# The routing of the second and third sequence begins one step later in the attention's list of steps

## The chip, the core and the metric

The kernel runs on one core of one Trainium2 chip. The metric is the device time of one execution in microseconds (us), the median of the runs. TensorE is called PE here, VectorE DVE, ScalarE ACT, GpSimd POOL and SyncE, whose queue issues most loads, SP.

## What is computed

Four sequences of 768 tokens with 8 heads of 64 go through windowed attention with four sink tokens. The result, 3072 rows of 512, goes through a mixture of 8 experts of which each token takes one, and then through one wide layer for all tokens. Cut to what matters:

```python
scores = scale * np.matmul(q, k.transpose(0, 1, 3, 2))
scores = np.where(is_sink | in_window, scores, -1000000000.0)
a = np.exp(scores - max); a = a / (sum + 1e-09)
x = np.matmul(a, v)                       # (4, 8, 768, 64) -> (3072, 512)

logits = x @ w_gate + modality_bias[modality_id]
e_idx = np.argmax(logits, axis=1)         # one of 8 experts for each token
out[mask] = gate_w[mask, None] * (np.maximum(x[mask] @ w1[e], 0.0) @ w2[e])

h = out @ w_in
out = (h * np.clip(h + 3.0, 0.0, 6.0) / 6.0) @ w_out
```

## The kernel before

**Stages.** The attention of 32 heads (4 sequences of 8) comes first and ends at about 225 us, the expert slots follow to about 590 us, and the wide layer fills the rest. All matmuls of the last two stages are TensorE's. The order on PE, DVE, ACT and POOL is the order in which the program writes the instructions; each engine works through its own list.

**A head.** `attend(n)` writes the steps of three heads at once: the scores of head n in three groups of two blocks (`scores_mm`, line 247), their maxima on DVE (`scores_max`, lines 261 to 272) and exponentials on ACT (`scores_exp`, lines 280 and 283); the transposes of head n-1's probabilities in two groups of three (`p_transpose`, line 318) with copies on ACT (`p_copy`, line 333) and masks on POOL; and the values of head n-2 (`values_mm`, lines 351 to 356). The normalisation of head n-3 (lines 361 to 373) stands inside the first maximum. Line 324 transposes a small block of sink values into the fourth quarter of the first group's buffer, and ACT copies that on line 328.

**Free slots.** Between the steps `attend` leaves six empty places (`None`). They are: ahead of the second scores, ahead of the first two values, ahead of the next two, ahead of the third scores, ahead of the last two values, and at the end of the head. At each of them one entry is taken from each of three lists: `side` (routing), `early` (start-up), `slow` (weights of the first expert and the first gather).

**Routing.** `route(b)` returns the routing of sequence b as a list of entries, each a list of small functions. `start(b)` puts that list into `side`, from the slot on that comes next; what is left of the former sequence's list is merged entry by entry. It is called ahead of heads 11, 19 and 27 for sequences 0, 1 and 2 and behind the loop for sequence 3. For each of the six blocks of 128 tokens the list has `txa` (four transposes of the attention's output `xb` on PE, line 393), one entry later `txb` (copy on ACT, line 398), one later `txc` (DVE subtracts the copy from the original, line 402); a block starts every three entries. `lga` are the gate's matmuls (line 410), `lgb` and `lgc` turn the result, `lgd` and `t1` to `t4` make the one-hot and gate value on DVE (lines 428 to 449, the one-hot on 443), `rk` counts ranks on PE (lines 456 and 459), `t5` and `t6` turn them into places (lines 464 to 470), `sx` and `keep` scale and store the rows (lines 476 to 483), `sc` scatters token numbers from POOL (line 494).

**The buffers.** `p_transpose`, `txa` and later the gathered rows' transposes (line 764) all write to tiles named `tp` of pool `pt`, which has two buffers in PSUM. A tile can be written when all readers of the one before in its buffer are done: ACT's copies of lines 333 and 328 for a `p_transpose`, ACT's copy of line 398 and DVE's subtraction of line 402 for a `txa`.

**Behind the loop.** What is left in `side` and `slow` becomes `rest`, of which six entries are taken at each step of the first expert slots. Line 701 is the second half of splitting a weight into a high and a low part (line 699 the first), on DVE or POOL; line 736 gathers token rows from POOL; lines 782 and 803 are the experts' matmuls.

Of the kernel before, what the change touches and what calls it, by code (L numbers as in the profile page):

```python
# [54 lines left out]
class Net:  # L55
# [321 lines left out]
    def route(self, b):  # L377
# [3 lines left out]
        q = []  # L381
# [118 lines left out]
        q = [[] for _ in range(ROUTED + late + 2 + 5 * (3, 2, 3, 1)[b])]  # L500
# [8 lines left out]
        for i in range(NB):  # L509
            q[33 + (1 if b == B - 1 else 2) * i].append(on(sx, i))  # L510
            q[(34 if b == B - 1 else 35) + (1 if b == B - 1 else 2) * i].append(on(keep, i))
            q[ROUTED + late + 1 + (3, 2, 3, 1)[b] * i].append(on(sc, i))
        return q

    def spread(self, places, n, most, move):

# [1147 lines left out]
```

## Time and profile before

| | us |
|---|---|
| median of 3 runs | 1120.08 |
| the runs | 1115.91 to 1120.35 |
| the profiled execution | 1115.64 |
| its span, first to last instruction | 1113.8 |
| PE busy | 1077.7 (97%) |
| DVE busy | 480.9 (43%) |
| ACT busy | 454.0 (41%) |
| POOL busy | 256.3 (23%) |

The span is cut into stretches to see where PE does not work. A row of the timeline is one instruction or several equal ones in a row, with the start, the duration and, in brackets, how long the engine was idle before it and what is thought to have ended that. PE's instructions overlap, so a group of them may end after the next has begun.

### The profile page before, as it was taken

The numbers are of one execution on the slowest core, as the hardware profiler recorded it, in microseconds if no ns is written. First come the engines' busy times: TensorE is split into PE (matmuls) and PEld (weight loads), VectorE is DVE, ScalarE is ACT, GpSimd is POOL, SyncE is SP. The second block draws the span as 40 slices with busy tenths as digits, with TensorE's granted clock in tenths as the row PEclk, the third lists the DMA queues.
The fourth block names the chain that finished last, engine by engine and source line by source line (L and its number), as shares of the span: only waits on it lengthen the run. The fifth ranks groups of instructions, "written<-read, shape, count | busy, mean of one in ns | idle before, by whom it ended". The sixth has DMA issues, their size and how long they took to land.

```text
span 1113.8 us, 18248 instructions
## 1 busy us (share of the span) xinstructions
PE 1077.7 (97%) x6805; PEld 988.8 (89%) x6805; DVE 480.9 (43%) x1271; ACT 454.0 (41%) x1111; POOL 256.3 (23%) x458
## 2 busy tenths in 40 slices
PE   8999999899999999999999999999999999999995
PEld 5998888798999987999988998989989989899894
DVE  5766869655544543742242422413314224133240
ACT  4555656544265645633252422413314224143140
POOL 3333536436142533442031000000000000000000
PEclk9999999999999999999999999999999999999998
DMA  6333778515786996772341010110101100100000
GB/s 189 107 111 90 161 152 165 106 57 106 152 241 187 268 278 218 174 193 87 64 124 38 21 38 10 30 38 8 31 10 30 38 11 29 33 7 20 10 11 22
DMA packets 59890, 102.07 MB, mean 92 GB/s; under 512 B 17552, under 2 KB 34576, under 8 KB 59792
## 3 DMA queue, kind: packets, MB, share of 16 engines
q1 hardware_dynamic: 39966, 74.16, 25.5%
q0 software_dynamic: 5840, 13.13, 4.8%
q10 hardware_dynamic: 13986, 13.53, 4.8%
q8 instruction: 55, 0.90, 0.4%
q14 instruction: 43, 0.35, 0.1%
HBM read 72.87 MB, written 27.92 MB: 90 GB/s over the span
## 4 chain that ended last, share of the span: by engine, by line
PE 56%; DVE 0%; DMA 0%; SPq 0%; issue 0%; POOL 0%; POOLq 0%; ACT 0%; DVEq 0%; ACTq 0%
PE mm L1084 24%; PE mm L1062 24%; PE mm L803 4%; PE mm L782 3%; DMA stg<-w_d 0%; PE tp L764 0%; DVE ga L1052 0%; SPq L1033 0%; DVE u L1067 0%; DVE ot L1090 0%; POOL out_dram L1098 0%; POOLq L1486 0%; DVE h L785 0%; ACT r L1065 0%; DVE cve L905 0%
## 5 line engine op out<-in xcount | busy, mean ns | idle before, releaser
L1062 PEld LDWEIGHTS mm<-yh,w 128*128 128x128 f32 x2304 | 274.6, 189 | 3.8 <-DVE u L1067 3.0
L1062 PE MATMUL mm<-yh,w 128*128 128x256 f32 x2304 | 275.0, 281 | 2.8 <-DVE u L1067 2.8
L1084 PE MATMUL mm<-w,ga 128*128 128x512 f32 x936 | 220.6, 394 | 0.1
L1084 PEld LDWEIGHTS mm<-w,ga 128*128 128x128 f32 x936 | 175.2, 188 | 39.9 <-DVE u L1067 0.3
L1065 ACT ACTIVATE r<-mm,b 128x256 f32<-128x256 f32 x192 | 91.2, 475 | 247.1 <-PE mm L1062 246.6
L803 PE MATMUL mm<-h,w 128*128 128x400 f32 x768 | 152.0, 351 | 2.4 <-POOL apart L493 2.2
L782 PE MATMUL mm<-xT,w 128*128 128x400 f32 x768 | 144.8, 347 | 2.0 <-ACT hT L842 1.6
L803 PEld LDWEIGHTS mm<-h,w 128*128 128x128 f32 x768 | 139.2, 190 | 4.1 <-POOL apart L493 2.6
L782 PEld LDWEIGHTS mm<-xT,w 128*128 128x128 f32 x768 | 139.7, 188 | 3.5 <-ACT hT L842 1.8
L1067 DVE SCALAR_TENSOR_TENSOR u<-r,mm 128x256 f32<-128x256 f32 x192 | 80.8, 421 | 140.0 <-ACT r L1065 139.6
L1098 POOL DMA_INDIRECT out_dram<-ot,idt x24 | 23.1, 962 | 491.4 <-ACT ot L1092 368.9
L1090 DVE COPY ot<-mm 128x512 f32<-128x512 f32 x12 | 8.3, 691 | 222.0 <-PE mm L1084 222.0
L247 PE MATMUL s<-kz,qq 128*128 128x260 f32 (+1 forms) x384 | 94.8, 369 | 4.6 <-ACT pr L283 2.6
L283 ACT ACTIVATE pr<-s,mn 128x132 f32<-128x132 f32 x160 | 52.3, 369 | 68.7 <-DVE mn L272 29.0
L701 POOL TENSOR_TENSOR w<-stg,w 128x512 fp32r<-128x512 f32 x35 | 47.1, 1350 | 131.3 <-ACT w L699 121.6
L247 PEld LDWEIGHTS s<-kz,qq 128*128 128x128 f32 x384 | 61.9, 191 | 10.2 <-ACT pr L283 3.3
L785 DVE SCALAR_TENSOR_TENSOR h<-mm,h 128x400 fp32r<-128x400 f32 x64 | 36.7, 573 | 74.1 <-ACT h L784 68.6
L1052 DVE SCALAR_TENSOR_TENSOR ga<-u,ga 128x256 fp32r<-128x256 f32 x156 | 67.2, 431 | 0.0
L1051 ACT ACTIVATE ga<-u 128x256 fp32r<-128x256 f32 x156 | 63.8, 409 | 1.1 <-DVE u L1067 1.1
L354 PE MATMUL o<-vt,pt5p 128*128 128x66 f32 x320 | 61.9, 275 | 0.0
L353 PE MATMUL o<-vt,pt5d 128*128 128x66 f32 x320 | 60.6, 271 | 0.0
L784 ACT ACTIVATE h<-mm 128x400 fp32r<-128x400 f32 x64 | 32.1, 502 | 69.7 <-PE mm L782 60.2
(228 smaller groups left out, 1236.9 us busy)
## 6 DMA issues: line engine op xcount, KB each, us to landing
stg<-w SPq DMA_DIRECT2D x16, 512.0 KB
cv<-w_in SPq DMA_DIRECT2D x16, 512.0 KB
w_d<-cva SPq DMA_DIRECT2D x32, 256.0 KB
cv<-w_out SPq DMA_DIRECT2D x16, 512.0 KB
stg<-w_d SPq DMA_DIRECT2D x16, 512.0 KB
yT_d<-y ACTq DMA_DIRECT2D x8, 800.0 KB
vt<-vv SPq DMA_DIRECT2D x16, 396.0 KB
kz<-kE SPq DMA_DIRECT2D x32, 197.0 KB
```

The source lines that it names most:

```text
L247: nc.tensor.matmul(s[:, a, :n], q[:, b], k[:, c:c + n], start=True, stop=True)
L283: self.nc.scalar.activation(pr[:, i], s[:, a, P:P + W], AF.Exp, bias=mn[:, i:i + 1], scale=-1.0)
L353: mm(o[:, j], d[:, j - 1], vt[:, j], start=False, stop=False)
L354: mm(o[:, j], p[:, j - 1], vt[:, j - 1], start=False, stop=False)
L782: nc.tensor.matmul(ph[:, :T1], w(k)[:, wi, c], xT[:, xi, k], start=(n == 0), stop=(n == 11))
L803: nc.tensor.matmul(py[:, :T1], wf[:, wi], h[:, hi, f], start=(n == 0), stop=(n == 23))
L1051: nc.scalar.mul(g(0, f), u, 1.0 / 6.0)
L1052: nc.vector.scalar_tensor_tensor(g(1, f), u, 1.0 / 6.0, g(0, f).bitcast(F32), ALU.mult, ALU.subtract)
L1062: nc.tensor.matmul(ph[:, :T2], w, yh[:, b, k], start=(n == 0), stop=(n == 11))
L1065: nc.scalar.activation(r, ph[:, :T2], AF.Relu, bias=self.b3)
L1067: nc.vector.scalar_tensor_tensor(u, r, 6.0, ph[:, :T2], ALU.min, ALU.mult)
L1084: nc.tensor.matmul(po, g(a, f)[:, t * P:(t + 1) * P], w[:, b], start=(n == 0), stop=(n == 47))
```

## The change

`route(b)` returns its list with one empty entry in front for sequences 1 and 2. The lists of sequences 0 and 3 are as they were.

```diff
-        return q
+        return [[]] * (b in (1, 2)) + q
```

All routing steps of the two sequences so move to the next free slot. The number of instructions of every engine is the same.

PE, head 20, the second head of sequence 1's routing (`kz_144` are its keys). Before:

```order
L247 MATMUL s<-kz_144,qq 128x128
L247 MATMUL s<-kz_144,qq 128x260
L318 MATMUL tp<-ident,pr 128x128 x3
L324 MATMUL tp<-ident,sk 128x128
L393 MATMUL tp<-ident,xb 128x128 x4
L247 MATMUL s<-kz_144,qq 128x260 x2
L318 MATMUL tp<-ident,pr 128x128 x3
```

After:

```order
L247 MATMUL s<-kz_144,qq 128x128
L247 MATMUL s<-kz_144,qq 128x260
L318 MATMUL tp<-ident,pr 128x128 x3
L324 MATMUL tp<-ident,sk 128x128
L247 MATMUL s<-kz_144,qq 128x260 x2
L318 MATMUL tp<-ident,pr 128x128 x3
L393 MATMUL tp<-ident,xb 128x128 x4
```

The four transposes of an even block have moved behind the second scores and the second group of probability transposes. Those of the odd block move in the same way from ahead of the third scores to behind them.

DVE, from head 19 into head 20 (`xt` is the routing's split copy, `mn` the maxima of the scores). Before:

```order
L402 TENSOR_TENSOR xt<-tp,xt 128x4x128
L361 TENSOR_SCALAR rc<-o 128x6
L261 ISA t_1930,mn<-s,m_165 128x128
L261 ISA mn 128x1
L366 RECIPROCAL rc<-rc 128x6
L373 TENSOR_TENSOR xb<-o,rc 128x6x64
L265 COPY_PREDICATED s<-up,s 128x128
L266 TENSOR_REDUCE mn<-s 128x1
```

After:

```order
L361 TENSOR_SCALAR rc<-o 128x6
L261 ISA t_1929,mn<-s,m_165 128x128
L261 ISA mn 128x1
L366 RECIPROCAL rc<-rc 128x6
L373 TENSOR_TENSOR xb<-o,rc 128x6x64
L265 COPY_PREDICATED s<-up,s 128x128
L266 TENSOR_REDUCE mn<-s 128x1
L402 TENSOR_TENSOR xt<-tp,xt 128x4x128
```

The subtraction for the odd block has moved behind the whole first maximum and normalisation of head 20.

ACT, from head 27 into head 28, with the split of an expert's weights (line 699). Before:

```order
L398 CAST xt<-tp 128x4x128
L283 ACTIVATE pr<-s,mn 128x132 x2
L398 CAST xt<-tp 128x4x128
L699 CAST w<-stg 128x512
L280 ACTIVATE pr<-t_2710,mn 128x128
```

After:

```order
L398 CAST xt<-tp 128x4x128
L283 ACTIVATE pr<-s,mn 128x132 x2
L699 CAST w<-stg 128x512
L398 CAST xt<-tp 128x4x128
L280 ACTIVATE pr<-t_2709,mn 128x128
```

The copy for the odd block has moved behind the weight cast that followed it.

## Rows read from the trace of the kernel before

**Rows 1.** Page, busy PE; then stretches: us, busy us (x) per engine, PEclk, DMA.
```profile
PE 1077.7 (97%) x6805; PEld 988.8 (89%) x6805; DVE 480.9 (43%) x1271; ACT 454.0 (41%) x1111; POOL 256.3 (23%) x458
...
150.00:200.00 50.00, 47.23 (x349) 42.79 (x349) 38.96 (x131) 31.52 (x85) 24.83 (x63) 1.00 0.75 150
200.00:250.00 50.00, 46.97 (x339) 43.56 (x338) 29.05 (x97) 21.91 (x58) 21.58 (x50) 1.00 0.29 86
```

**Rows 2.** Timeline of PE: start, us, engine, line, operation, tiles, count, idle before.
```profile
139.39 0.63 PE L393 MATMUL tp<-ident,xb 128*128 128x128 f32 x4 [0.86 <-DVE rc L361]
...
147.34 0.63 PE L393 MATMUL tp<-ident,xb 128*128 128x128 f32 x4 [0.20 <-PE tp L324]
...
172.30 0.19 PE L456 MATMUL l<-r_ohz,tri 128*128 128x56 bf16 x1 [0.63 <-DVE r_ohz L443]
...
196.75 0.63 PE L393 MATMUL tp<-ident,xb 128*128 128x128 f32 x4 [1.63 <-issue]
...
206.00 0.63 PE L393 MATMUL tp<-ident,xb 128*128 128x128 f32 x4 [1.49 <-DVE rc L361]
```

**Rows 3.** Timeline of ACT and DVE at the start of head 28.
```profile
195.30 0.58 ACT L398 CAST xt<-tp 128x512 fp32r<-128x512 f32 x1
...
195.91 0.69 DVE L402 TENSOR_TENSOR xt<-tp,xt 128x512 fp32r<-128x512 f32 x1 [1.23 <-ACT pr L283]
```

**Rows 4.** Timeline of head 23, which has no routing transposes.
```profile
161.53 0.82 PE L247 MATMUL s<-kz,qq 128*128 128x128 f32 x4
...
162.62 1.04 PE L247 MATMUL s<-kz,qq 128*128 128x260 f32 x4
...
163.45 0.27 ACT L328 CAST skt<-tp 128x128 fp32r<-128x128 f32 x1
163.50 0.49 PE L318 MATMUL tp<-ident,pr 128*128 128x128 f32 x3
...
163.83 0.34 PE L351 MATMUL o<-vt,pt6a 128*128 128x66 f32 x2
163.84 0.42 DVE L269 COPY_PREDICATED s<-up,s 128x256 f32<-128x256 uint32 x1
```

**Rows 5.** Timeline of PE: first scores and first values of heads 20, 21, 22, 28, 29.
```profile
137.27 0.83 PE L247 MATMUL s<-kz,qq 128*128 128x128 f32 x4
...
141.06 0.34 PE L351 MATMUL o<-vt,pt6a 128*128 128x66 f32 x2
...
145.87 0.83 PE L247 MATMUL s<-kz,qq 128*128 128x128 f32 x4
...
149.25 0.34 PE L351 MATMUL o<-vt,pt6a 128*128 128x66 f32 x2
...
154.43 0.82 PE L247 MATMUL s<-kz,qq 128*128 128x128 f32 x4
...
156.74 0.34 PE L351 MATMUL o<-vt,pt6a 128*128 128x66 f32 x2
...
193.86 0.82 PE L247 MATMUL s<-kz,qq 128*128 128x128 f32 x4
...
198.43 0.34 PE L351 MATMUL o<-vt,pt6a 128*128 128x66 f32 x2
...
203.24 0.83 PE L247 MATMUL s<-kz,qq 128*128 128x128 f32 x4
...
207.67 0.34 PE L351 MATMUL o<-vt,pt6a 128*128 128x66 f32 x2
```

**Rows 6.** Timeline of DVE: the one-hot of sequence 1.
```profile
172.05 0.20 DVE L443 TENSOR_TENSOR r_ohz<-r_pr,r_pm 128x48 bf16<-128x48 f32 x1
```

**Rows 7.** Timeline of PE behind the attention; then two stretches, PEclk as in group 1.
```profile
267.08 0.64 PE L803 MATMUL mm<-h,w 128*128 128x400 f32 x1 [2.23 <-POOL apart L493]
...
195.00:198.00 3.00, 1.37 (x10) 1.09 (x9) 2.02 (x8) 2.33 (x7) 0.16 (x1) 1.00 0.68 51
268.00:270.00 2.00, 2.00 (x7) 1.98 (x8) 1.86 (x13) 1.04 (x3) 0.56 (x1) 0.50 0.46 177
```

## The prediction

> **What bounds the kernel now.** I read the page first: TensorE is busy 97% of the span, and in the two stretches that hold the routing of the second and third sequence it is still busy 47.23 and 46.97 of 50 us [rows 1]. So time moves only where TensorE waits, and all that these 100 us can give back is the 5.8 us it does not work. The list of PE's waits shows where that lies. Four of them are the same wait: 0.86 and 0.20 us in heads 20 and 21, 1.63 and 1.49 us in heads 28 and 29 [rows 2], 4.18 us together. Each stands before four transposes of the attention's output (line 393, "txa" below). The releaser's name there is no guide: what the transposes need is a free buffer of the two in pool `pt`, and the one they get is held by the transposes before them until DVE has subtracted (line 402, "txc"). In head 28 the copy on ACT starts at 195.30, the subtraction ends at 195.91 + 0.69 = 196.60, and PE goes on at 196.75 [rows 2, 3]: 0.15 us from end to release. So the chain is: exponentials, copy, subtraction, PE.
>
> I write T for the start of a head's first scores, and count from T to the start of the head's values (line 351), behind which PE is packed before and after.
>
> **What the change does there.** One empty entry in front of the list moves every routing step one slot later in the head. txa of an even block goes from ahead of the second scores to behind the transposes of the probabilities (line 318); its copy goes one slot on; txc of the odd block goes from a head's last slot to the next head's first, which on DVE is behind the maximum of line 266. Nothing is added or removed. PE meets the transposes of the probabilities earlier and asks for the contested buffer later, but the subtraction that frees it also comes later. The sum is the race between the two.
>
> **PE's side.** Head 23 has no routing transposes, so it shows the bare times: T = 161.53, the second scores at T+1.09, the transposes at T+1.97, the values at T+2.30 [rows 4]. The transposes take 0.33 us of issue. One txa takes 0.46: in head 20 the values start 1.67 us after it (141.06 - 139.39) [rows 2, 5], of which the second scores are 0.88 and the transposes 0.33. So after the change PE would want the buffer at T+2.30 and without any wait start the values at T+2.76.
>
> **DVE's side.** In head 23 the operation behind line 266 starts at 163.84 = T+2.31 [rows 4]. That becomes the place of txc: it ends at T+2.31+0.69 = T+3.00 and releases PE at T+3.15. So the wait is not gone. txa starts at T+3.15 and the values at T+3.61.
>
> **ACT's side, a new wait.** Where txa stood between, the transposes of line 318 had time to wait for the buffer that the first group of transposes used, freed by ACT's copy of line 328. Now they meet it bare: that copy ends at 163.72 = T+2.19 [rows 4], release at T+2.34, against T+1.97 for PE. In heads 20, 21 and 29 this 0.37 lies inside the wait to T+3.15. In heads 22 and 30, whose txa are over, it stands alone: there the late txc of the last block still holds the other buffer when they come, so they take the slow one, and the values start at T+2.34+0.33 = T+2.67. In head 28 the transposes get the buffer of the late txc instead: T+3.15+0.33+0.46 = T+3.94.
>
> **The sum**, values before against after [rows 5], T subtracted:
> head 20: 141.06-137.27 = 3.79 against 3.61, gain 0.18.
> head 21: 149.25-145.87 = 3.38 against 3.61, loss 0.23.
> head 22: 156.74-154.43 = 2.31 against 2.67, loss 0.36.
> head 28: 198.43-193.86 = 4.57 against 3.94, gain 0.63.
> head 29: 207.67-203.24 = 4.43 against 3.61, gain 0.82.
> head 30: built as head 22, loss 0.37.
> Together a gain of 0.67 us. Heads 28 and 29 pay most before because ACT and DVE also split expert weights there; heads 21 and 22 lose because their old waits were shorter than the new ones. The weak terms are 28 and 29. If their exponentials come as late as now, ACT's queue (exponentials, a weight cast that now stands ahead of the copy, copy, then the pieces that line 328 waits behind) can give back their whole 1.45 us: the sum is then a loss of 0.8. If ACT comes early enough that heads 22 and 30 meet no wait, the gain is 1.4. I take 0.67, since the work on DVE ahead of the third scores' maximum is the same and only its order changes.
>
> **The rank matmuls** of the second sequence (line 456) wait 0.63 us for the one-hot that DVE makes at 172.05 [rows 2, 6]. They move behind the third scores, 0.88 us of PE work (163.50 - 162.62 in head 23) [rows 4]. But the one-hot comes later too: lines 432, 433, 437 and 439 and a weight split now stand behind the maxima of the head's first and second scores and in front of it, and no row says whether that is more or less than 0.88. I count 0; the ends are the whole wait gone, a gain of 0.63, and as much again, a loss of 0.63. For the third sequence these matmuls lie behind the loop, in the same step.
>
> **What is moved past, at nothing.** Behind the loop the leftover list is popped six at a time and is 29 entries before, 30 after: five steps both times, so the tables, gathers and weight loads stay where they are. The first slot's token load and gather queue behind the weight splits in the other list, which is not shifted. SP swaps the order of two loads, POOL issues four scatters half a head later; PE is covered by 8 us of attention for either. If the scatters came late, the 2.23 us that PE waits at 267.08 [rows 7] would grow with them.
>
> Here a rule of the Trainium skill bears, "Perfetto Trace Analysis", section Optimization Strategy: a gap that repeats can mean that there is no free buffer for the next tile. By it, with still two buffers in the pool, the gap would only move and the sum be 0 in place of 0.67. The four like waits of group 2 agree with its diagnosis.
>
> **Numbers.** The profiled execution took 1115.64 us, its span 1113.8; with the sum it is 1115.0. The median of the runs shown is 1120.08 (1115.91 to 1120.35), and 0.7 less gives 1119.4. A difference under 0.5%, 5.6 us, can't be told from none here.
>
> **Rivals.**
> *The waits vanish.* If copy and subtraction were done before PE asks, all of groups 2 and 6 would go: 4.18 + 0.63 = 4.81 us, 1115.3. For it: PE asks about one microsecond later than now. Against: so does DVE, and even in a head with nothing else in it txc's place comes only at T+2.31 [rows 4].
> *Every head pays the longest wait.* The late subtraction sits ahead of the maxima of the second scores, and so ahead of ACT's exponentials, the copies behind them and the next subtraction. If this feeds itself from head to head, each of the six heads waits as head 28 does now: 6 x 1.63 = 9.78 us against 4.18, slower by 5.6, 1125.7. It decides where txc releases PE later than about T+3.9 (T+2.30 + 1.63). For it: heads 28 and 29 are there already. Against: in head 23 DVE has slack, and one subtraction is 0.69.
> *A wait trips TensorE's clock.* After the 2.23 us wait the granted clock is 0.50 for 268 to 270, the lower of the two levels (1.2 of 2.4 GHz); after the 1.63 us wait it stays 1.00 [rows 7]. At half speed 2 us lose 1.0; once is 1120.4, once in each of four heads 1123.4. No wait that I expect is longer than 1.2 us, so little speaks for it.
>
> **Chances.** The forecast, between 2 us faster and 2 slower, 0.74; waits vanish 0.09; every head pays 0.09; clock or something unseen behind the loop 0.08. Of the first two nothing passes 0.5% by itself, of the third half, and the unseen can go either way: faster 0.06, same 0.87, slower 0.07. The range reaches down to the vanished waits and the lowest run shown less the gain, and up to the clock's price, leaving out the far ends: 1114.0 to 1123.5.
>
> **What would show it.** Right: PE waits of 0.8 to 1.2 us in front of line 393 or 318 in heads 20, 21, 28 and 29, released 0.15 us after a txc; new waits of 0.3 to 0.4 in heads 22 and 30; the rank wait about as long; the end of attention within 2 us of where it is. Wrong: no wait in these heads, or values later than T+4 in several, or a change behind the loop larger than in it.

## The result, and the profile after

| | before | after |
|---|---|---|
| median, us | 1120.2 | 1130.5 |
| lowest and highest, us | 1115.9 to 1122.7 | 1129.3 to 1137.2 |
| profiled execution, us | 1115.64 | 1130.89 |
| its span, us | 1113.8 | 1129.1 |

The ratio of the runs is 1.012, with a 95% interval of 1.009 to 1.015: 1.2% slower, where I forecast 1119.4 us, in a range of 1114.0 to 1123.5, and no change that can be told. On another chip the changed kernel was again slower than the kernel before run beside it, there by 0.75% (1.0075, 1.0045 to 1.0105).

The page of the kernel after, and the two stretches that answer to [rows 1]:

```profile
PE 1089.0 (96%) x6805; PEld 996.2 (88%) x6805; DVE 481.4 (43%) x1271; ACT 454.6 (40%) x1111; POOL 257.1 (23%) x458
```

```profile
150.00:200.00 50.00, 44.04 (x315) 38.19 (x313) 32.31 (x112) 26.92 (x75) 21.07 (x53) 0.97 0.58 143
200.00:250.00 50.00, 46.34 (x323) 41.53 (x324) 32.06 (x104) 24.74 (x69) 20.03 (x50) 0.96 0.32 63
```

DVE's and ACT's work is the same. PE has the same 6805 instructions, yet is busy 11.3 us longer, of the 15.3 us that the span has grown: the granted clock has fallen to 0.97 and 0.96, where it was 1.00 in both stretches, and matmuls last longer at a lower clock (line 247 for two blocks: 1.04 us at 1.00 [rows 4], 2.10 at 0.50 below). So what is lost is waiting and, behind it, slower matmuls. The starts of the heads tell where. The table gives how much longer a head is than in the kernel before, worked out from the starts of its first and the next head's first scores (line 247). Beside the profile of the result it has the forecast and two runs that are told of below: the changed kernel again, and with six buffers for the scaled rows (the second of the two runs of that).

| head | forecast | after | after again | six buffers |
|---|---|---|---|---|
| 20 | -0.18 | +4.57 | -0.21 | -0.21 |
| 21 | +0.23 | +0.19 | +0.21 | +0.20 |
| 22 | +0.36 | +0.34 | +0.34 | +0.34 |
| 23 to 26 | 0 | +0.13 | +0.15 | +0.46 |
| 27 | 0 | **+7.45** | **+5.08** | +0.81 |
| 28 | -0.63 | -0.59 | -0.59 | -0.60 |
| 29 | -0.82 | -0.86 | -0.85 | -0.84 |
| 30 | +0.37 | +0.35 | +0.35 | +0.35 |
| sum | -0.67 | +11.58 | +4.48 | +0.51 |

The six heads that the forecast priced came out as priced, but for head 20 in the profile of the result. The loss is head 27, which the forecast did not list, and in that one profile head 20. Of the other 3.7 us of the span, 1.40 lie ahead of head 20, where nothing was changed, and 2.3 behind head 30.

PE's waits in the kernel after, from head 20 to head 29, which answer to [rows 2]:

```profile
142.76 0.86 PE L318 MATMUL tp<-ident,pr 128*128 128x128 f32 x3 [1.96 <-ACT skt L328]
154.88 0.66 PE L393 MATMUL tp<-ident,xb 128*128 128x128 f32 x4 [0.23 <-DVE xt L402]
179.86 0.19 PE L456 MATMUL l<-r_ohz,tri 128*128 128x56 bf16 x1 [0.63 <-DVE r_ohz L443]
195.55 0.33 PE L324 MATMUL tp<-ident,sk 128*128 128x128 f32 x1 [0.53 <-POOL apart L493]
200.37 2.10 PE L247 MATMUL s<-kz,qq 128*128 128x260 f32 x4 [4.49 <-ACT pr L283]
...
211.07 0.52 PE L318 MATMUL tp<-ident,pr 128*128 128x128 f32 x3 [0.99 <-DVE xt L402]
...
219.77 0.65 PE L393 MATMUL tp<-ident,xb 128*128 128x128 f32 x4 [0.23 <-DVE xt L402]
```

The waits for the contested buffer, 0.20, 1.63 and 1.49 us in heads 21, 28 and 29 before, are now 0.23, 0.99 and 0.23; the 1.96 us of head 20 have another cause, told below. The 0.63 us is that of the rank matmuls, and the 0.53 us of head 27 is new. The large new wait is 4.49 us at 200.37: the second scores of head 27 wait for exponentials. ACT's timeline there says what ACT was doing (ACTq is a DMA that ACT issues):

```profile
188.45 0.34 ACTq L483 DMA_DIRECT2D xs_d<-xs  x1
...
192.21 0.67 ACT L283 ACTIVATE pr<-s,mn 128x132 f32<-128x132 f32 x2
198.56 0.72 ACT L476 ACTIVATE xs<-xb,r_gt 128x512 f32<-128x512 f32 x1 [5.68 <-DMA xs_d<-xs]
199.19 0.60 ACT L699 CAST w<-stg 128x512 fp32r<-128x512 f32 x1
199.70 0.62 ACT L283 ACTIVATE pr<-s,mn 128x132 f32<-128x132 f32 x2
```

The six row blocks of a sequence are scaled and stored one after the other; DVE scales the first, third and fifth (line 478), ACT the second, fourth and sixth (line 476). Here line 476 scales the sixth block of sequence 1. It stands ahead of a weight cast and of the two exponentials, and it stood idle for 5.68 us: there are three buffers for scaled rows, and the one it needs is free when the store of the third block (line 483, issued at 188.45) has landed. That store took 198.56 - 188.45 = 10.1 us to land. SP's loads there, of the next heads' keys, queries and values (197 + 384 + 396 KB):

```profile
186.56 0.47 SPq L211 DMA_DIRECT2D kz<-kE  x1
187.09 0.58 SPq L215 DMA_DIRECT2D qq<-qT  x1
187.76 0.38 SPq L221 DMA_DIRECT2D vt<-vv  x1
```

The store was issued 0.69 us behind them. In the kernel before, ACT's and then SP's rows of the same place are:

```profile
179.90 0.34 ACTq L483 DMA_DIRECT2D xs_d<-xs  x1
...
185.92 0.72 ACT L476 ACTIVATE xs<-xb,r_gt 128x512 f32<-128x512 f32 x1
```

```profile
180.04 0.47 SPq L211 DMA_DIRECT2D kz<-kE  x1
180.56 0.58 SPq L215 DMA_DIRECT2D qq<-qT  x1
181.23 0.50 SPq L221 DMA_DIRECT2D vt<-vv  x1
```

There the third store was issued 0.14 us ahead of the loads, and 6.0 us later, when the sixth scaling came, its buffer was free. One slot was enough to change the order. The wait costs more than itself, because TensorE's clock falls with it (after; columns as in [rows 1]):

```profile
195.00:200.00 5.00, 0.35 (x2) 0.14 (x1) 0.18 (x1) 1.44 (x4) 2.54 (x6) 0.75 0.50 36
200.00:205.00 5.00, 4.63 (x21) 4.14 (x21) 3.53 (x14) 3.71 (x11) 1.98 (x5) 0.57 0.58 60
```

PE works 0.35 of the 5 us from 195 to 200, and in the next 5 us its clock is 0.57; from 198 to 204 it is 0.50, the lower of its two levels (1.2 of 2.4 GHz). Head 27 took 6.62 us before, and PE was busy for all of them; after, it takes 14.07, of which PE is busy for 9.05. So of the 7.45 us that it is longer, 5.02 are idle time and 2.43 are the same matmuls at the lower clock.

Head 20 shows a stop of another kind in this profile. DVE's row there:

```profile
141.29 0.16 DVE L361 TENSOR_SCALAR rc<-o 128x6 f32<-128x6 f32 x1 [3.01 <-PE s L247]
```

The values that line 361 needs were started by PE at 138.43 for 0.40 us, and I found no other operand missing, yet DVE goes on only at 141.29, 2.62 us after the head's start. Behind it the clock is 0.53 from 145 to 150. I come back to it.

### The profile page after: what moved, and what is told of

Same layout as the page of the kernel before. It is cut to its first block, busy times and chain, and to the rows that moved or that the text cites. A ratio compares the mean times of both kernels' runs of the same rounds, so it can differ in the third digit from the quotient of the medians.

```text
span 1129.1 us, 18242 instructions
## 1 busy us (share of the span) xinstructions
PE 1089.0 (96%) x6805; PEld 996.2 (88%) x6805; DVE 481.4 (43%) x1271; ACT 454.6 (40%) x1111; POOL 257.1 (23%) x458
## 4 chain that ended last, share of the span: by engine, by line
PE 54%; DMA 1%; SPq 0%; DVE 0%; issue 0%; ACTq 0%; POOL 0%; POOLq 0%; ACT 0%
PE mm L1084 24%; PE mm L1062 23%; PE mm L803 4%; PE mm L782 3%; DMA ids_d<-ti 1%; SPq L1033 0%; DMA stg<-w_d 0%; PE tp L764 0%; DVE ot L1090 0%; POOL out_dram L1098 0%; ACTq L869 0%; DVE y L808 0%; POOLq L1486 0%; DVE h L785 0%; ACT r L1065 0%
## 5 line engine op out<-in xcount | busy, mean ns | idle before, releaser
L247 PE MATMUL s<-kz,qq 128*128 128x260 f32 (+1 forms) x384 | 98.3, 379 | 7.3 <-ACT pr L283 6.7
L336 POOL TENSOR_SCALAR_AFFINE_SELECT pt5d<-pt6a 128x256 f32<-128x256 f32 x64 | 31.4, 491 | 137.2 <-ACT pt6a L333 137.1
```

The costliest lines, as they stand in the source:

```text
L247: nc.tensor.matmul(s[:, a, :n], q[:, b], k[:, c:c + n], start=True, stop=True)
```

## Experiments

Each group of kernels was timed on one chip with the kernel before beside it (medians of 1109.9 to 1111.6 us). A ratio is the time of a kernel over that of the kernel before beside it, with its 95% interval; head lengths and waits are from the one profiled execution of each kernel.

**Which sequence.** First the empty entry for one sequence alone, `[[]] * (b == 1) + q`:

> Only sequence 1's list has the empty entry; sequence 2's is as before. After the change the starts of the heads fall back in two places, both while sequence 1's list runs: 4.57 us in head 20, where DVE stands still 3.01 us ahead of line 361, and 7.45 us in head 27, where ACT's scaling of a row block (line 476) stands 5.68 us for a store to land, ahead of two exponentials that PE needs. Theory: both belong to sequence 1's list, and sequence 2's part of the change gains the 1.1 us that heads 28 to 30 show. Then this kernel is at 1130.5 + 1.1 = 1131.6. Rival: a good part is behind the loop (the last transposes, gathers and scatters come later), that is sequence 2's: then 1121 to 1126.

Measured: 1.0035 (1.0009 to 1.0061). ACT waited 5.20 us in front of line 476 and PE 3.57 us behind it; head 27 was 8.48 us longer. Head 20 did not stop. The expected 1131.6 was in the first chip's times; as a ratio it is 1.0%, of which 0.4 were head 20's 4.57 us, and these did not come. The ratio is also worth only 3.9 us: the ten runs go from 1112.1 to 1119.1, and the profiled one, 1118.5, is among the longest, so most executions lose less than the profile shows. Then `[[]] * (b == 2) + q`:

> Only sequence 2's list has the empty entry; sequence 1's is as before. Theory: what is lost belongs to sequence 1's list, so this kernel has no stop in heads 20 and 27 and gains about 1.1 us in heads 28 to 30: 1119 (1118 to 1120.5). Rival (loss behind the loop): 1125 or more, with longer waits of PE in front of lines 764 and 803 than the 2.23 us of before.

Measured: 0.9978 (0.9957 to 0.9999), and a second time:

> Sequence 2's list alone shifted, once more. Theory: the gain of heads 28 to 30 (1.1 us in the profile of the changed kernel, 0.67 + 0.41 forecast for these three heads) is all that it does: 0.1% faster than before, at most 0.25%. Rival: the 0.22% of the first time was chance, 0.

Measured: 1.0000 (0.9985 to 1.0016). In the attention no scaling stood for a store for more than 0.4 us in either. So the loss is sequence 1's, and the gain of sequence 2 is in its heads but too small to be told in the time.

**The wait taken away.** In the changed kernel more buffers:

```diff
-            xs = self.rx.tile([P, DM], F32, name="xs", bufs=3)
+            xs = self.rx.tile([P, DM], F32, name="xs", bufs=6)
```

> The changed kernel with six buffers for the scaled rows (line 474) in place of three, so that no scaling has to wait for a store of the same sequence. Theory: ACT's 5.68 us wait in head 27 is that store, and with it the 4.49 us wait of PE and the half clock behind it go: about 7.4 us less than the changed kernel, 1123, and head 20 keeps its 4.6. Rival (PE's wait in head 27 is the contested buffer of the transposes, or the store only landed late because something else held ACT): the time stays near 1130.

Measured: 1.0004 (0.9979 to 1.0028). No row of line 476 waits for a store, and head 20 did not stop. A second time:

> The changed kernel with six buffers for the scaled rows, once more. Its profile of the first time lost 1.26 us from head 23 to head 28 and gained 0.78 in the other heads of the change: 0.5 us in all, 0.04% slower than before. If the 0.2 to 0.3% of the kernels with four buffers and with early stores is the true rest, it is 0.2% or more slower here too.

Measured: 1.0007 (0.9993 to 1.0022). The changed kernel itself:

> The changed kernel once more, on the chip of the experiments. Theory: the stop of head 27 comes again (7 to 8.5 us in the profile, as it did with sequence 1 alone), the 4.57 us of head 20 do not, since three kernels with the same list up to there did not show it: 0.2% slower than the kernel before (the 0.35% of sequence 1 alone less the 0.2% that sequence 2 gained). Rival: both stops belong to the change: 1.2% slower, as on the first chip.

Measured: 1.0075 (1.0045 to 1.0105); ACT waited 3.74 us in front of line 476, PE 2.53, and head 27 was 5.08 us longer. That is less than expected in head 27 and more in the time (0.2%). With six buffers 0.04 and 0.07% of the 0.75% are left, and 0.51 of the 4.48 us in the table: about nine tenths of the loss go with the store's wait. Head 20 lost nothing here, so the stop there is not needed for the change to be slower. Four buffers:

> The changed kernel with four buffers for the scaled rows: the sixth scaling takes the buffer of the second, whose store is issued 2.6 us ahead of the third's and ahead of the loads. Theory: it has landed in time, no scaling waits, and the time is that of six buffers (0 to 0.1% from the kernel before). Rival: that store is late as well, a wait of 2 us or more stays, 0.3% or more slower.

Measured: 1.0021 (1.0003 to 1.0038), without a wait for a store in sequence 1, but 0.1% above what was expected. The control, the kernel before with six buffers:

> The kernel before with six buffers for the scaled rows. Theory: there no scaling of sequences 0 to 2 waited for a store in the profile, so nothing is gained in the attention: within 0.1% of the kernel before. Rival: in some executions the store is late there too, and the lower median would show it: 0.2% or more faster.

Measured: 0.9988 (0.9974 to 1.0003): the buffers alone do nothing that can be told. Nor do six buffers with sequence 2 alone moved:

> Only sequence 2's list has the empty entry, and six buffers for the scaled rows. Theory: the gain of heads 28 to 30 stays (1.1 to 1.5 us) and nothing else changes: 0.1 to 0.2% faster than the kernel before, as sequence 2 alone was. Rival: the 0.2% there was chance; 0.

Measured: 0.9996 (0.9984 to 1.0009). In its profile the gain is not there: head 28 is 4.40 us longer than before, by a stop of ACT without a store in it, told of under head 20 below.

**Which step.** The changed kernel with scalings and stores in their old slots, and the kernel before with only these one entry later:

```diff
-            q[33 + (1 if b == B - 1 else 2) * i].append(on(sx, i))
+            e = b in (1, 2)
+            q[33 + e + (1 if b == B - 1 else 2) * i].append(on(sx, i))
```

(the same `e` for the stores; with a minus sign in the changed kernel).

> The changed kernel, but the scalings of the rows and their stores (lines 476 to 483) of sequences 1 and 2 are put one entry earlier in the list and so keep their old slots; all else stays one slot late. Theory that it is the place of the scaling in ACT's queue, ahead of the last exponentials of the head, that costs: head 27 loses nothing, 1123. Rival: the store lands late because of what else is being loaded at that time (a 512 KB weight load is issued at 180.00 us where it was 173.05 before), so the wait goes with it to the old slot: 1127 to 1131.

Measured: 1.0000 (0.9975 to 1.0025), that is, no loss; the third store is issued 0.25 us behind the first of the loads and ahead of the other two, and the sixth scaling 5.7 us later finds its buffer free.

> The kernel before, and of sequences 1 and 2 only the scalings of the rows and their stores (lines 476 to 483) one entry later; the transposes, the gate and the ranks stay in their old slots. Theory: this alone brings the stop of head 27 (7.5 to 8.5 us where the store of the buffer lands late, as in the changed kernel and in the kernel with sequence 1 alone shifted), and none of the gains of heads 28 and 29: 0.3 to 0.8% slower than the kernel before, and the profile shows ACT's line 476 waiting for a store. Rival: it takes the late copies and subtractions too, which change when ACT and the loads come; then this kernel is within 0.1% of the kernel before and no line 476 waits.

Measured: 1.0061 (1.0044 to 1.0077). Its timeline, ACT, then PE:

```profile
180.65 0.39 ACTq L483 DMA_DIRECT2D xs_d<-xs  x1
...
191.52 0.72 ACT L476 ACTIVATE xs<-xb,r_gt 128x512 f32<-128x512 f32 x1 [5.81 <-DMA xs_d<-xs]
```

```profile
193.33 2.10 PE L247 MATMUL s<-kz,qq 128*128 128x260 f32 x4 [4.81 <-ACT pr L283]
```

The store, issued 0.02 us behind the last of the loads, lands after 10.9 us. Head 27 is 10.08 us longer. Moving the scalings and their stores is enough. The price is above the 7.5 to 8.5 us expected. The same with six buffers:

> The kernel before with only the scalings and stores of sequences 1 and 2 one entry later, and six buffers. Theory: without the store's wait the late scalings cost what their place ahead of the exponentials costs, about the 1.26 us that heads 23 to 28 lost in the changed kernel with six buffers: 0.1% slower than before. Rival: those 1.26 us are from the other moved steps; then 0, and all of the 0.61% of the kernel with three buffers was the store.

Measured: 0.9992 (0.9979 to 1.0006), and heads 23 to 27 together are as long as before to 0.02 us. So the late scalings cost nothing that shows but the store's wait. The 1.27 us which these heads lose in the changed kernel with six buffers belong to the other moved steps, as does the 0.95 us that they lose where the scalings keep their old slots. Two rows of the second run with six buffers (PE, heads 26 and 27) show most of it; before, line 247 waited 0.30 us there and line 324 not at all:

```profile
184.69 1.15 PE L247 MATMUL s<-kz,qq 128*128 128x260 f32 x4 [0.73 <-ACT pr L283]
191.17 0.33 PE L324 MATMUL tp<-ident,sk 128*128 128x128 f32 x1 [0.54 <-POOL apart L493]
```

**Why the store is late.** Is it slow anyway, or slow behind the loads? The kernel before, its routing not moved, with `bufs=2`:

> The kernel before, its routing not moved, with two buffers for the scaled rows in place of three, so that the fourth to sixth scaling of a sequence has to wait for the store of two blocks earlier and shows when it lands. In the profiles so far the late store was issued 0.0 to 0.7 us behind the loads of the next pair of heads (lines 211 to 221, 977 KB on SP's queue) and landed 8.2 to 10.9 us after its issue; where it was issued ahead of them no scaling waited, 5.5 to 6.0 us after. Theory: stores queue behind the loads; here too those issued ahead of the loads land in under 6 us and those issued right behind them in 8 to 11, and the stop comes without any moved routing: 0.5 to 1.2% slower than before. Rival: a store of this size always takes 8 to 11 us here; then each of the waits in sequence 1 shows that.

Measured: 1.0185 (1.0154 to 1.0216). Sequence 1, ACT, DVE and SP:

```profile
185.94 0.34 ACTq L483 DMA_DIRECT2D xs_d<-xs  x1
...
189.94 0.34 ACTq L483 DMA_DIRECT2D xs_d<-xs  x1
191.21 0.34 ACTq L483 DMA_DIRECT2D xs_d<-xs  x1
192.11 0.72 ACT L476 ACTIVATE xs<-xb,r_gt 128x512 f32<-128x512 f32 x1 [1.59 <-DMA xs_d<-xs]
192.93 0.34 ACTq L483 DMA_DIRECT2D xs_d<-xs  x1
...
205.07 0.72 ACT L476 ACTIVATE xs<-xb,r_gt 128x512 f32<-128x512 f32 x1 [6.03 <-DMA xs_d<-xs]
```

```profile
190.69 0.49 DVE L478 TENSOR_SCALAR xs<-xb,r_gt 128x512 f32<-128x512 f32 x1 [0.84 <-DMA xs_d<-xs]
194.53 0.48 DVE L478 TENSOR_SCALAR xs<-xb,r_gt 128x512 f32<-128x512 f32 x1 [1.83 <-DMA xs_d<-xs]
```

```profile
190.65 0.47 SPq L211 DMA_DIRECT2D kz<-kE  x1
191.17 0.58 SPq L215 DMA_DIRECT2D qq<-qT  x1
191.84 0.38 SPq L221 DMA_DIRECT2D vt<-vv  x1
```

Each scaling that waits starts when a store has landed, so four landings can be read, in one sequence of one kernel. The stores issued at 185.94, 189.94 and 191.21, ahead of or among the loads, landed 4.8, 2.2 and 3.3 us later; the one issued at 192.93, behind all three, landed 12.1 us later. Sequence 0 has the same stop in its own last scaling (7.96 us on ACT, 6.90 on PE, store 12.1 us after its issue), in a head that is 9.06 us longer; with two such stops the kernel lost more than expected. The rival, that a store always takes 8 us or more, falls.

Then the changed kernel with the stores in their old slots and the scalings late:

> The changed kernel with the stores of sequences 1 and 2 (line 483) one entry earlier, which is the slot they have in the kernel before, and the scalings one slot late as in the changed kernel. Theory: the third store is then issued ahead of the loads of the next pair of heads, as before, lands in under 6 us, and the sixth scaling, one slot later than before, finds its buffer free: no wait, no more than 0.1% slower than before. Rival: the store takes 8 to 11 us wherever it is issued; then the wait shrinks only by the one slot, to 2 to 4 us, and some 0.4% stay.

Measured: 1.0028 (1.0010 to 1.0046). The third store goes out at 181.29, 0.03 us ahead of the first load, and the sixth scaling starts at 187.89 without a wait. The mechanism is as expected, the time 0.2% above the 0.1% expected.

Last, is it ACT's own queue that is late, or any store behind the loads? In the changed kernel POOL issues sequence 1's stores:

```diff
-            nc.scalar.dma_start(out=self.xs[n * P:(n + 1) * P, :], in_=r["xs", i])
+            (nc.gpsimd if b == 1 else nc.scalar).dma_start(out=self.xs[n * P:(n + 1) * P, :], in_=r["xs", i])
```

> The changed kernel with the six stores of sequence 1 (line 483) issued by POOL instead of ACT, so through POOL's queue; three buffers. Theory that the loads hold the DMA engines: the third store lands 8 us or more after its issue again, ACT's line 476 waits 3 to 6 us and the kernel is 0.5 to 0.9% slower than before. Rival, that it is ACT's queue that is late: the store lands in under 6 us, no wait, within 0.2%.

Measured: 1.0132 (1.0113 to 1.0152). POOL, then DVE:

```profile
184.88 0.59 POOL L483 DMA_DIRECT2D xs_d<-xs  x1
```

```profile
194.03 0.48 DVE L478 TENSOR_SCALAR xs<-xb,r_gt 128x512 f32<-128x512 f32 x1 [7.25 <-DMA xs_d<-xs]
```

POOL issues its stores later, so here it is already the second store that lies behind the loads (the last of them at 184.41). It lands after 9.15 us, and now DVE stands for it; the loss is larger than expected. POOL's first store, issued at 181.33 ahead of the loads, had landed when the fourth scaling asked for its buffer 4.57 us later. So it is not a matter of ACT's queue alone. This agrees with the Trainium skill, "DMA: Bandwidth & Descriptors", section Issuing engines are not separate DMA queues: transfers that different engines start run on the same DMA engines. The section also says that they interleave; of that the changed kernel's profile shows nothing from 188.50 to 191.00, just behind the third store's issue, where the queue of SP's loads moved 0.64 MB and ACT's queue had no packet.

All kernels together: issued ahead of or among the loads, the third store had landed by the time its buffer was asked for, 5.7 to 6.6 us later, in every kernel with three buffers; issued 0.02 to 0.70 us behind the last load it took 8.2 (the changed kernel again), 9.6 (sequence 1 alone), 10.1 and 10.9 us.

**A faster version** was not found: no kernel here is faster than the kernel before by an amount that held twice.

## Why the prediction was wrong

- **Contested buffer, PE's and DVE's side: right.** In the changed kernel run again, head 20's first scores and values are

```profile
137.26 0.82 PE L247 MATMUL s<-kz,qq 128*128 128x128 f32 x4
...
140.79 0.34 PE L351 MATMUL o<-vt,pt6a 128*128 128x66 f32 x2
```

  that is T+3.53, where T+3.61 was worked out; heads 21 and 29 have T+3.53 too. Head 28 has T+3.92 for 3.94, heads 22 and 30 T+2.65 and 2.64 for 2.67. The weak terms, 28 and 29, held: -0.59 and -0.85 for -0.63 and -0.82. The six heads sum to -0.75 us for -0.67. The sign that was named, waits of 0.8 to 1.2 us in front of line 393 or 318, came in head 28 alone (0.99). In heads 20, 21 and 29 the row has 0.23, for the transposes ahead started at T+2.26, not T+1.97, and count as work until T+2.81; the subtraction still decided, as forecast.
- **The rule that a repeating gap can mean that no buffer is free** (the Trainium skill, "Perfetto Trace Analysis", section Optimization Strategy): by it the prediction put a sum of 0 beside its own 0.67. The six heads gave back 0.75 us with the same two buffers, since the late step asks later. The diagnosis was right, the conclusion drawn from it here was not.
- **Rank matmuls: right, by luck.** 0.63 before [rows 2], 0.63 after, at 179.86. That the late ask and the late one-hot cancel was counted without a row for it, so this is luck.
- **"What is moved past, at nothing": this is the step that failed.** It went through the leftover list, the gather queue, SP and POOL, but not through the stores that ACT issues and the buffers that they hold. The scaling on ACT moved one slot too, and with it the store three blocks before, from ahead of the loads to behind them. A term put at 0 cost 5.08 to 10.08 us, the loss of head 27. The "order of two loads" on SP was seen, and not that a store of ours would change places with loads. The trace of before had such rows, in sequence 3 (ACT):

```profile
269.89 0.72 ACT L476 ACTIVATE xs<-xb,r_gt 128x512 f32<-128x512 f32 x1 [0.96 <-DMA xs_d<-xs]
...
272.00 0.72 ACT L476 ACTIVATE xs<-xb,r_gt 128x512 f32<-128x512 f32 x1 [1.39 <-DMA xs_d<-xs]
```

  They show that three buffers can be too few. The 6.0 us from the third store to the sixth scaling, against loads that go out 0.14 us behind that store, were in it as well.
- The same step counted what else moves as covered: waits of 0.73 us in head 26 (0.30 before) and 0.54 us in head 27 (none before) were not. This is small against the rest.
- **Behind the loop:** 2.3 us more than before in the profile of the result. The wait that was 2.23 [rows 7] is 2.67, but in fourteen of the seventeen profiles here it is 2.05 to 2.72, moved or not, and in the other three no wait there passes 1.2, so I read nothing from it.
- **The rival "a wait trips TensorE's clock": its mechanism came, its premise was wrong.** "No wait that I expect is longer than 1.2 us" was true of those I expected. Head 27 has one of 2.53 to 4.81 us, and the clock behind it was at its lower level each time, for 3 to 9 us.
- **The rival "every head pays the longest wait"** (1125.7) has a loss of the right sign, but its cause did not come: the waits of line 393 shrank.
- **The median:** 10 us longer on the first chip; in the profiled execution head 27 is 7.45 and head 20 4.57 us longer.
- **The range:** its lower end, 1114.0, is said to come from the vanished waits and the lowest run less the gain, but these are 1115.3 and 1115.2. It made no difference here.

**Head 20, half open.** In the nine profiles in which sequence 1's list is moved, line 361 of head 20 starts 0.20 us after the head's first scores in six, and 1.56, 2.07 and 2.62 us after them in three (early stores, four buffers, the result). It is no effect of the change: in the second run with sequence 2 alone moved, whose list is the old one there, DVE had the row

```profile
141.53 0.17 DVE L361 TENSOR_SCALAR rc<-o 128x6 f32<-128x6 f32 x1 [0.78 <-PE tp L324]
```

at 2.76 us. But in the old order the subtraction of line 402 stands ahead of line 361 until 1.98 us, and hides most of such a stop: that head was 0.83 us longer, against 4.57 in the result. That the move takes this cover away is argued from the order; no run was made for it. The prediction put the late subtraction's own time on the path and did not ask what it had hidden. I found no operand that line 361 waited for, and why DVE stops there isn't shown. It is not DVE's alone, nor this head's: with six buffers and sequence 2 alone moved, ACT's copy of line 398 started at 193.49 after 2.54 us of idle time, though the transposes that it copies had been started at 189.02 for 0.62 us, and PE's clock was 0.50 from 200 to 205.

**What stays open.** Whether that stop came in the other runs of the first chip can't be told, so the difference between 1.2% there and 0.75% later has no shown cause. Of the 0.75%, 8.3 us, the profile has 4.48 in the table's heads; the six runs go from 1116.0 to 1125.8, and the profiled one, 1117.15, is among the shorter. Four buffers and early stores stay 0.2 and 0.3% above the kernel before, six buffers 0.04 and 0.07%: in these two profiles head 20 is 1.07 and 0.56 us longer, 0.1% at most, and the rest I can't explain. Why a store behind the loads takes 8 to 12 us is only half shown (last section).

## What to carry to other kernels

When a list of steps moves by one slot, go through the DMAs that the steps issue and not only through the instructions: for each, which buffer it holds, which instruction waits for it to land, and what stands behind that instruction on its engine. A store's landing time isn't a constant; look whether large loads go out just ahead of it or just behind, for a slot can swap them. Where the interval from a store to the next use of its buffer is close to the landing time, look at more buffers first: here six took the wait away and left nothing that can be told of the loss, and issuing the stores from POOL did not help.

## What the runs showed of the hardware

The landing time of a 256 KB store went from 2.2 to 4.8 us (elsewhere at most 6.6) to 8.2 to 12.1 us, by its place among 977 KB of loads: issued 0.63 us ahead of the last load it took 3.3 us, 0.02 us behind it 10.9. The bytes don't explain that. In the changed kernel the third store was issued at 188.45. Until 191.00 only the loads moved, 0.64 MB; from 191.00 to 193.50 ACT's queue moved 0.66 of the 0.79 MB of the three stores then on it (issued at 188.45, 189.89 and 191.89); its last 0.11 MB took until 198.5. So about half of the 10.1 us went by behind the loads and with the bulk of the three stores, and the other half in a slow tail. These two stretches show the fast and the slow phase, and of the second the queue that ACT's stores use (packets, MB, share of the time of 16 DMA engines):

```profile
192.00:193.00 1.00, 1.00 (x8) 0.88 (x7) 0.65 (x2) 0.88 (x3) 0.59 (x2) 1.00 0.99 368
194.00:198.00 4.00, 1.35 (x9) 0.82 (x7) 0.00 (x0) 0.00 (x0) 3.48 (x8) 0.93 0.81 47
```

```profile
q10 hardware_dynamic: 49, 0.08, 48.9%
```

At 368 GB/s these 0.08 MB would take 0.2 us; they took most of 4 us, with 47 GB/s in all, while the DMA engines counted as 0.81 busy. Which of the three stores they belong to isn't shown.

What makes the tail slow wasn't tried, and one rival to the loads stands: POOL's scatters (line 494), whose first packets in this burst move from 191.5 on, with the late stores. In the kernel before, no whole microsecond from 60 to 131 moves under 120 GB/s with the DMA engines over 0.6 busy, though loads as large run there, and none from 145 to 187; the 16 such between 131 and 203 all lie behind the first of a sequence's scatters (issued at 124.64 and 181.44). In the kernel after the 12 such from 60 to 217 lie the same way. That scatters were moved is not what makes a store late: with only the scalings and stores moved they kept their slots (the first at 181.48), and the store took 10.9 us. But each late store here was still on its way when a sequence's scatters ran, so how much of the tail is theirs and how much comes of the loads is open.
